# Transposed x by token tiles in DRAM and stored over six stages, attention tiles on the right side of SBUF, last stores on SyncE

## The chip, the cores and the metric

The kernel runs on one core of a Trainium2 chip. The metric is the device time of one execution in microseconds, the median over several executions. The timed number is about 1.8 us longer than the span of the same execution in its profile (for one execution of the changed kernel 1546.8 against 1545.1 us), so a span and a time are never compared with each other here.

## The reference

One transformer-like block on 2048 tokens of width 1024 in bf16: a layer norm, a segment-recurrent attention (32 heads of 128, segments of 32 tokens, 8 memory tokens carried from segment to segment), and an MLP-mixer branch, added to x. Cut to what matters here:

```python
def _A_ref(x, mem0, Wq, Wk, Wv, Wo, seg_len):      # x is the layer-normed input
    ...
    for s in range(n_seg):                         # 64 segments of 32 tokens
        h = concatenate([mem, xs], axis=1)         # 8 memory rows + 32 tokens
        q, k, v = h @ Wq, h @ Wk, h @ Wv           # 32 heads x 128
        p = softmax(mask(q k^T * scale))
        o = (p v) @ Wo
        mem = o[:, :M]
        outs.append(o[:, M:])
...
return x + _A_ref(xn, ...) + _B_ref(xn, w1, w2, w3, w4)
```

## The kernel before

The kernel has these stages, with their times in its trace: layer norm and the mixer branch (to about 545 us), the projection to V (545 to 771 us), attention in five groups of token blocks, (0), (1), (2), (3) and (4, 5), each over eight groups of heads (771 to about 1495 us), and the output projection with its closing checks. Four parts matter.

The V stage multiplies the transposed x, which lies in SBUF as `xT`, with eight slices of Wv. The results go through `Vs` buffers to DRAM on the SyncE queue. In the second of the eight steps the whole `xT` is also stored to DRAM, on the GpSimd queue, because its SBUF space is given up afterwards:

```python
vsp = vctx.enter_context(tc.tile_pool(name="vsp", bufs=3, side="right"))
...
for hg in range(8):
    ...                                            # loads of Wv, and of Wo for 1 <= hg < 5, on GpSimd
    for m4 in range(4):
        Vs = vsp.tile([P, 4, 512], BF16, tag="Vs")
        for j in range(4):
            ps = psum.tile([P, 512], F32, tag="mm", bufs=4)
            for k in range(KT):
                nc.tensor.matmul(ps[:], xT[:, m4 * 4 + j, k, :], wv[:, k, :], ...)      # L569
            if j % 2 == 0:
                nc.scalar.copy(Vs[:, j, :], ps[:])                                      # L571
            else:
                nc.vector.tensor_copy(Vs[:, j, :], ps[:])
        nc.sync.dma_start(V_d[...], Vs[:])
    if hg == 1:
        ...
        for n in range(NT):                        # 16 stores of 256 KB in a burst
            nc.gpsimd.dma_start(xT_d[:, :, n * P:(n + 1) * P], xT[:, n])                # L579
```

Attention reads the transposed x back, block by block of 384 tokens (the last block has 128), in 18 DMAs on GpSimd. `block_setup` for the next group is written in the third step of the group before, so almost a whole group ahead of its use:

```python
def block_setup(b):
    ...
    elif b == 5:
        nc.gpsimd.dma_start(hTb[:, :, 0:96], xT_d[:, :, a:a + 96])                      # L603
        nc.gpsimd.dma_start(hTb[:, :, 99:131], xT_d[:, :, a + 96:a + 128])              # L604
        nc.vector.tensor_copy(hTb[:, :, 96:99], MZ[:, :, 67:70])                        # L605
        nc.vector.tensor_copy(hTb[:, :, 131:132], MZ[:, :, 70:71])                      # L606
        ...
    else:
        for i in range(4):
            nc.gpsimd.dma_start(hTb[:, :, i, 0:96], xT_d[:, :, a + 96 * i:a + 96 * (i + 1)])   # L612
...
if hg == 2 and gi_ + 1 < len(groups):
    nextB = {b: block_setup(b) for b in groups[gi_ + 1]}
```

The two small copies at L605 and L606 put columns for the memory rows into the tile of block 5. They run on VectorE, which also does part of the softmax.

The weights of the next step of attention are loaded on SyncE, in two halves each, and SyncE also issues the transposes of the softmax weights P:

```python
for k0 in (0, 4):
    loads.append(lambda ...: nc.sync.dma_start(w[:, k0:k0 + 4, :], src[:, k0:k0 + 4, cs_]))    # L724
...
nc.sync.dma_start_transpose(PTr, Pn[:rows]...)                                          # L669
```

The results are stored on GpSimd, piece by piece, the last two pieces at the very end:

```python
nc.vector.tensor_tensor(ot[:], self.ps[:], self.Rt[:], op=ALU.add)                      # L703
nc.gpsimd.dma_start(out_v[:, self.gi, self.cc], ot[:])                                  # L704
```

Of the kernel before, what the change touches and what calls it, by code (L numbers as in the profile page):

```python
# [15 lines left out]
BF16 = mybir.dt.bfloat16  # L16
# [7 lines left out]
P = 128  # L24
S = 2048
D = 1024
KT = D // P
NT = S // P
# [49 lines left out]
def kernel(  # L78
# [16 lines left out]
    nc = tc.nc  # L95
    x_v = A_x[0].rearrange("(n p) d -> p n d", p=P)
    out_v = out[0].rearrange("(n p) d -> p n d", p=P)
# [12 lines left out]
    R1_v = R1_d.rearrange("(n p) d -> p n d", p=P)  # L110
    xn_d = tc.dram_tile([S, D], BF16, name="xn_scratch")
    xn_v = xn_d.rearrange("(n p) d -> p n d", p=P)
    xT_d = tc.dram_tile([P, KT, S], BF16, name="xT_scratch")
    V_d = tc.dram_tile([S, H * DH], BF16, name="V_scratch")
    Vr_d = tc.dram_tile([NQ + 1, H * DH], BF16, name="Vmem_scratch")

# [41 lines left out]
    def tiles_of(b):  # L158
        if b == 5:
            segs = (3, 1)  # L160
        else:
            segs = (3, 3, 3, 3)
        out_, c, t0 = [], 0, 4 * b
        for i, s in enumerate(segs):
            first = b == 0 and i == 0
            nm = s + (M - 1 if first else 0)
            msk = mask_first if first else (mask_reg if s == 3 else mask_last)
            r0 = 0 if first else 7 + 3 * (t0 + i)
            out_.append(dict(c0=c, ntok=s * SEG, nm=nm, T=s * SEG + nm, mask=msk, r0=r0, tok=i * 96, i=i, gi=t0 + i))
            c += s * SEG + nm  # L170
        return out_, c

    def fill(hTb, tl, x_of):

        for t in tl:
            a = t["tok"]
            end = a + t["ntok"]
            while a < end:
                j, o = divmod(a, P)
                w = min(P - o, end - a)  # L180
                d = t["c0"] + a - t["tok"]
                nc.vector.tensor_copy(hTb[:, :, d:d + w], x_of(j)[:, :, o:o + w])
                a += w
            d = t["c0"] + t["ntok"]
            nc.vector.tensor_copy(hTb[:, :, d:d + t["nm"]], MZ[:, :, t["r0"]:t["r0"] + t["nm"]])

    with tc.manual_schedule(engines={mybir.EngineType.PE, mybir.EngineType.SP, mybir.EngineType.Pool}), ExitStack() as actx:
        wpool = actx.enter_context(tc.tile_pool(name="aw", bufs=4, side="right"))

        def wtile():  # L190
            return wpool.tile([P, KT, 512], BF16, tag="w", name="wt")

        psum = actx.enter_context(tc.tile_pool(name="psum", bufs=4, space=PSUM))
        with ExitStack() as bctx:
# [13 lines left out]
            with ExitStack() as hctx:  # L208
# [161 lines left out]
                with ExitStack() as p2:  # L370
                    ring = p2.enter_context(tc.tile_pool(name="p2ring", bufs=4))
                    for n in range(NT):
                        x1 = ring.tile([P, D], F32, tag="x1")
                        st = ring.tile([P, 2, 6], F32, tag="st")
                        for ch in range(2):
                            ps = psum.tile([P, 512], F32, tag="mm", bufs=4)
                            for k in range(KT):
                                o = 2 + n * P + SH[k]
# [5 lines left out]
                        a = ring.tile([P, 1], F32, tag="a")  # L384
# [12 lines left out]
            with ExitStack() as p3:  # L397
# [97 lines left out]
                def load_wv():  # L495
                    hg = len(wvs)
                    if hg < 8:
                        wvs.append(wtile())
                        nc.gpsimd.dma_start(wvs[-1][:], Wv_v[:, :, hg * 512:(hg + 1) * 512])
# [10 lines left out]
                for tb in range(4):  # L510
# [12 lines left out]
                    if tb == 3:  # L523
# [4 lines left out]
                        xT = vph.tile([P, NT, KT, P], BF16)  # L528
                    for j in range(4):
                        n = tb * 4 + j  # L530
# [26 lines left out]
            for hg in range(8):  # L557
                cs_ = slice(hg * 512, (hg + 1) * 512)
                while len(wvs) < min(8, hg + 3):
                    load_wv()  # L560
                wv = wvs[hg]
                if 1 <= hg < 5:
                    nc.gpsimd.dma_start(wo_sb[:, (hg - 1) * 8:hg * 8, :], Wo_v[:, (hg - 1) * 8:hg * 8, :])
# [5 lines that stand above are left out]
                            nc.tensor.matmul(ps[:], xT[:, m4 * 4 + j, k, :], wv[:, k, :], start=(k == 0), stop=(k == KT - 1))  # L569
# [4 lines that stand above are left out]
                    nc.sync.dma_start(V_d[m4 * 512:(m4 + 1) * 512, cs_].rearrange("(j p) c -> p j c", p=P), Vs[:])  # L574
                if hg == 1:
                    for t in pns:
                        nc.gpsimd.memset(t[:], 0.0)
                    for n in range(NT):
                        nc.gpsimd.dma_start(xT_d[:, :, n * P:(n + 1) * P], xT[:, n])  # L579
                if hg == 6:  # L580
                    first_w = [wtile(), wtile()]
                    for w, src in zip(first_w, (Wq_v, Wk_v)):
                        nc.sync.dma_start(w[:], src[:, :, 0:512])
                if hg == 0:
                    tl, nb = tiles_of(0)
                    hTb0 = early.tile([P, KT, 408], BF16, tag="hTb")
                    fill(hTb0, tl, lambda j: xT[:, j])
# [3 lines left out]
        apsum = actx.enter_context(tc.tile_pool(name="apsum", bufs=2, space=PSUM))  # L591
        smp = actx.enter_context(tc.tile_pool(name="asm", bufs=2))
        iop = actx.enter_context(tc.tile_pool(name="aio", bufs=2))
        qkv = actx.enter_context(tc.tile_pool(name="aqkv", bufs=2))
        def block_setup(b):
            tl, nb = tiles_of(b)
            ntok = sum(t["ntok"] for t in tl)
            a = 384 * b
            if b == 0:
                hTb, rhs = hTb0, lambda k: hTb0[:, k, :nb]  # L600
            elif b == 5:
                hTb = early.tile([P, KT, 136], BF16, tag="hT5", bufs=1)
                nc.gpsimd.dma_start(hTb[:, :, 0:96], xT_d[:, :, a:a + 96])  # L603
                nc.gpsimd.dma_start(hTb[:, :, 99:131], xT_d[:, :, a + 96:a + 128])  # L604
                nc.vector.tensor_copy(hTb[:, :, 96:99], MZ[:, :, 67:70])  # L605
                nc.vector.tensor_copy(hTb[:, :, 131:132], MZ[:, :, 70:71])  # L606
                rhs = lambda k: hTb[:, k, :nb]
            else:
                hTb = early.tile([P, KT, 4, 104], BF16, tag="hTb")
                r0 = tl[0]["r0"]  # L610
                for i in range(4):
                    nc.gpsimd.dma_start(hTb[:, :, i, 0:96], xT_d[:, :, a + 96 * i:a + 96 * (i + 1)])  # L612
                nc.vector.tensor_copy(hTb[:, :, :, 96:99], MZ[:, :, r0:r0 + 12].rearrange("p k (t r) -> p k t r", t=4))
                rhs = lambda k: hTb[:, k, :, 0:99]
                for i, t in enumerate(tl):
                    t["c0"] = 104 * i
            return dict(b=b, tiles=tl, nb=nb, ntok=ntok, rhs=rhs, cols=nb if b in (0, 5) else 416)
# [67 lines left out]
        class Out:  # L685
            def __init__(self, oX, gi, gl, ch):
                self.oX, self.gi, self.gl, self.cc, self.ps = oX, gi, gl, slice(ch * 512, (ch + 1) * 512), None
                self.late = False

            def piece(self, hg):  # L690
                if self.ps is None:
                    self.ps = psum.tile([P, 512], F32, tag="mm", bufs=4, name="pso")
                if hg == (6 if self.late else 0):
                    self.Rt = iop.tile([P, 512], F32, tag="Rt")
                    nc.gpsimd.dma_start(self.Rt[:], R_v[:, self.gi, self.cc])
                for h in range(4 * hg, 4 * hg + 4):
                    nc.tensor.matmul(self.ps[:], self.oX[:, h, self.gl * P:(self.gl + 1) * P], wo_sb[:, h, self.cc], start=(h == 0), stop=(h == H - 1))  # L697
                if hg == 7:
                    ot = iop.tile([P, 512], BF16, tag="ot")
                    if DEBUG_A:  # L700
                        nc.vector.tensor_copy(ot[:], self.ps[:])
                    else:
                        nc.vector.tensor_tensor(ot[:], self.ps[:], self.Rt[:], op=ALU.add)  # L703
                    nc.gpsimd.dma_start(out_v[:, self.gi, self.cc], ot[:])  # L704

        smalls = []
        clock = [0.0]
# [21 lines left out]
        def tick(us, blocked=None):  # L729

            clock[0] += us
            turn[0] += 1
            if turn[0] % every == 0:
                load_some(1)
            done = set()
            for item in list(smalls):
                due, kind, fn = item
                if due <= clock[0] and kind != blocked and kind[0] not in done and not (kind[0] == "S" and flying[0] >= 5):
                    smalls.remove(item)
                    flying[0] += 1 if kind[0] == "S" else -1  # L740
                    done.add(kind[0])
                    clock[0] += fn()
# [57 lines left out]
        head, rest = outs[:4], outs[4:]  # L800
        for o in head:
            o.late = True
        for p in range(6):
            for o in head:
                o.piece(p)
                tick(0.86)
# [45 lines left out]
    with tc.If(cond > 0):  # L852
        with ExitStack() as fctx:
# [18 lines left out]
            with tc.For_i(0, NSEG, 1) as i:  # L872
# [57 lines left out]
                ot = fr.tile([L, D], BF16, tag="ot")  # L930
# [50 lines left out]
```

## Time and profile before

| | before |
|---|---|
| median of 3 runs at the time of the prediction | 1542.9 us (1540.59 to 1543.96) |
| TensorE busy | 1514.8 of 1545.1 us |
| sum of TensorE's gaps over 0.5 us | 16.0 us, in 12 gaps |
| largest of them | 3.37 us at 594 us, in the V stage |

The last two rows are worked out from the trace's list of weight loads: a gap is the time from the end of one weight load to the start of the next. The last matmul still runs for a part of it, so the idle time of TensorE is 0.1 to 0.4 us shorter: 3.08 us in the largest gap. The prediction's 16 us are the same sum. In the same way, all gaps named below without a profile line are gaps between weight loads.

In the profile's lines PE is TensorE at its matmuls, PEld TensorE loading weights, ACT ScalarE, DVE VectorE, POOL GpSimd, and SPq the DMA queue of SyncE. The page's head gives the span, and its first part the busy time, share of the span and number of instructions of each engine:

```profile
span 1545.1 us, 25390 instructions
PE 1514.8 (98%) x10308; PEld 839.7 (54%) x10382; DVE 523.8 (34%) x1092; ACT 513.9 (33%) x1218; POOL 192.5 (12%) x272
```

TensorE is the limit: only what takes gaps from it, or puts gaps into it, can move the time. The matmul count is 10308 although 10382 weights were loaded. Some matmul records are missing from this trace, so its PE sum is a little low and isn't compared with that of another trace.

The list of waits names the waiting engine and tile, then what released it, then total us, number, and the longest:

```profile
ACT Vs L571 <- DMA V_scratch<-Vs: 21.7, 3, 9.8
...
ACT QT L647 <- DMA V_scratch<-Vs: 4.9, 1, 4.9
...
PE ps L569 <- ACT Vs L571: 3.1, 1, 3.1
...
PE ps L639 <- DMA wt<-in_A_Wq_dram: 1.3, 2, 0.6
```

The first and third lines belong together. ACT couldn't evict a V result because a store from `Vs` to DRAM hadn't freed its buffer, and TensorE then waited for that eviction. The timeline of TensorE shows where (start, length, line, output and inputs, count, and in brackets the wait ahead), and the windows below it show each engine's busy time, then the granted clock (the share of full speed that TensorE was given), DMA share and GB/s. The four windows are two around this wait and two at 1215 to 1235 us:

```profile
584.70 9.44 PE L569 MATMUL ps<-wt,xT 128*128 128x512 bf16 x42
597.23 8.97 PE L569 MATMUL ps<-wt,xT 128*128 128x512 bf16 x32 [3.08 <-ACT Vs L571]
```

```profile
core 0: us, PE busy (x) PEld busy (x) DVE busy (x) ACT busy (x) POOL busy (x), PEclk, DMA share, GB/s
585.00:595.00 10.00, 9.09 (x42) 4.02 (x42) 1.38 (x2) 1.07 (x2) 0.00 (x0) 1.00 0.98 278
595.00:605.00 10.00, 7.72 (x28) 3.21 (x29) 1.98 (x3) 2.25 (x4) 0.00 (x0) 0.83 0.82 295
1215.00:1225.00 10.00, 10.00 (x82) 6.35 (x80) 3.09 (x7) 5.96 (x17) 6.36 (x8) 1.00 0.79 152
1225.00:1235.00 10.00, 10.00 (x77) 6.18 (x75) 6.82 (x17) 5.55 (x15) 0.00 (x0) 1.00 1.12 233
```

A clock of 0.83 over 10 us is 3.4 us at half clock; it follows the gap, and costs half of its length.

GpSimd's timeline shows the burst of stores that filled the DMA engines, and much later its loads of x for the last group:

```profile
553.22 5.26 POOL L579 DMA_DIRECT2D xT_scratch<-xT  x6
560.73 0.84 POOL L579 DMA_DIRECT2D xT_scratch<-xT  x1 [2.26 <-DMA wt<-in_A_Wv_dram]
568.61 0.84 POOL L579 DMA_DIRECT2D xT_scratch<-xT  x1 [7.04 <-DMA wo_sb<-in_A_Wo_dram]
569.89 3.46 POOL L579 DMA_DIRECT2D xT_scratch<-xT  x4 [0.43 <-issue]
...
1215.36 0.55 POOL L704 DMA_DIRECT2D out_dram<-ot  x1 [5.83 <-DVE ot L703]
1215.89 3.52 POOL L612 DMA_DIRECT2D hTb<-xT_scratch  x4
1219.41 0.88 POOL L603 DMA_DIRECT2D hTb<-xT_scratch  x1
1220.28 0.88 POOL L604 DMA_DIRECT2D hTb<-xT_scratch  x1
```

SyncE's timeline at that place has the second half of Wq, 1.8 us after the last of GpSimd's six loads was issued (1220.28 + 0.88 = 1221.16). This order was not noticed before the prediction:

```profile
1222.99 0.57 SPq L724 DMA_DIRECT2D wt<-in_A_Wq_dram  x1
```

At the end of the kernel, the lines of the output stores and of the closing drain (engine, operation, count, shortest/median/longest in ns, then first and last start):

```profile
L704 POOL DMA_DIRECT2D out_dram<-ot x32: 540/545/560, 901.1 to 1540.1; - x32
```

```profile
L976 POOLq DRAIN  x3: 46/98/3166, 1541.1 to 1544.9; - x3
```

GpSimd issues its last store at 1540.1 us and then drains for 3.17 us.

### The profile page before, as it was taken

How to read it: one execution, taken by the hardware profiler on the slowest of the kernel's cores; microseconds unless marked ns; L12 is line 12 of the kernel's file. 1: busy time of each engine (PE TensorE's matmuls, PEld its weight loads, DVE VectorE, ACT ScalarE, POOL GpSimd, SP SyncE). 2: the span in 40 equal slices, each digit the busy share in tenths (PEclk: the TensorE clock that was granted, in tenths of full speed). 3: DMA queues.
4: the chain of work that ended last, by engine and by line, in shares of the span. 5: the costliest groups of instructions: out<-in, count | busy, mean ns of one | idle time of the engine just before them, and what ended most of it. 6: DMA issues, size and time to landing. Idle time of an engine off the chain costs nothing. (4 is left out here: it accounts for less than half of the span.)

```text
span 1545.1 us, 25390 instructions
## 1 busy us (share of the span) xinstructions
PE 1514.8 (98%) x10308; PEld 839.7 (54%) x10382; DVE 523.8 (34%) x1092; ACT 513.9 (33%) x1218; POOL 192.5 (12%) x272
## 2 busy tenths in 40 slices
PE   7999999999999999999999999999999999999998
PEld 7844444444444444444456645654665566466654
DVE  8284010000200111111246624651663365235541
ACT  5533202103012011111156614651662366056620
POOL 5232020221211241010000011002000200100001
PEclk9999999999999999999999999999999999999999
DMA  7679543452353998542389947992997599458611
GB/s 251 182 213 311 205 148 125 143 184 83 130 164 87 215 275 273 173 124 83 123 231 252 235 129 179 246 237 73 239 239 175 129 249 227 111 130 198 136 45 50
DMA packets 288601, 270.39 MB, mean 175 GB/s; under 512 B 137459, under 2 KB 255368, under 8 KB 288480
## 3 DMA queue, kind: packets, MB, share of 16 engines
q1 hardware_dynamic: 265088, 185.53, 47.0%
q0 software_dynamic: 23392, 83.19, 16.8%
q8 instruction: 83, 1.36, 0.4%
q14 instruction: 38, 0.31, 0.1%
HBM read 190.73 MB, written 46.73 MB: 154 GB/s over the span
## 5 line engine op out<-in xcount | busy, mean ns | idle before, releaser
L639 PE MATMUL ps<-hTb,wt 128*128 128x396 bf16 (+2 forms) x3072 | 514.9, 314 | 1.3 <-DMA wt<-in_A_Wq_dram 1.3
L639 PEld LDWEIGHTS <-wt 128*128 128x128 bf16 x3072 | 264.5, 97 | 148.1 <-DMA wt<-in_A_Wq_dram 2.1
L569 PE MATMUL ps<-wt,xT 128*128 128x512 bf16 x1004 | 222.0, 381 | 4.1 <-ACT Vs L571 3.1
L697 PE MATMUL pso<-wo_sb,oX 128*128 128x512 bf16 x1000 | 223.2, 379 | 1.4 <-issue 0.2
L515 PE MATMUL ps<-xn3T,w_sb 128*128 128x512 bf16 x896 | 195.9, 379 | 1.1 <-ACT h3T L516 1.1
L540 PE MATMUL ps<-w_sb,h3T 128*128 128x512 bf16 x872 | 194.3, 379 | 1.2
L569 PEld LDWEIGHTS <-xT 128*128 128x128 bf16 x1024 | 100.6, 98 | 125.3 <-issue 5.6
L516 ACT ACTIVATE h3T<-ps 128x512 bf16<-128x512 f32 x112 | 66.5, 597 | 292.0 <-PE ps L515 289.0
L697 PEld LDWEIGHTS <-oX 128*128 128x128 bf16 x1024 | 98.9, 98 | 115.3
L645 ACT CAST KT<-ps 128x396 bf16<-128x396 f32 (+1 forms) x192 | 87.1, 456 | 189.6 <-PE ps L639 186.5
L515 PEld LDWEIGHTS <-w_sb 128*128 128x128 bf16 x896 | 86.8, 98 | 103.9 <-issue 1.3
L540 PEld LDWEIGHTS <-h3T 128*128 128x128 bf16 x896 | 86.8, 98 | 102.8
L660 DVE TENSOR_REDUCE sums<-sm 99x4 f32<-99x396 f32 (+1 forms) x176 | 97.6, 555 | 113.9 <-ACT sm L658 113.9
L647 ACT ACTIVATE QT<-ps 128x396 bf16<-128x396 f32 (+1 forms) x192 | 89.4, 469 | 108.0 <-PE ps L639 79.8
L656 DVE TENSOR_TENSOR sm<-psS,c_mask_reg_sb 99x396 f32<-99x396 f32 x160 | 91.4, 572 | 90.1 <-PE psS L654 89.9
L571 ACT CAST Vs<-ps 128x512 bf16<-128x512 f32 x64 | 37.2, 586 | 238.4 <-PE ps L569 152.6
L658 ACT ACTIVATE sm<-sm 99x396 f32<-99x396 f32 (+1 forms) x176 | 92.7, 527 | 65.9 <-DVE sm L656 64.7
L573 DVE CAST Vs<-ps 128x512 bf16<-128x512 f32 x64 | 44.2, 692 | 181.8 <-PE ps L569 156.8
L666 DVE TENSOR_TENSOR Pn<-sm,rs 99x396 bf16<-99x396 f32 (+1 forms) x176 | 99.0, 562 | 10.2 <-DMA PT<-Pn 4.0
L541 DVE TENSOR_TENSOR R<-ps,R 128x512 f32<-128x512 f32 x32 | 22.1, 692 | 231.4 <-PE ps L540 215.0
L704 POOL DMA_DIRECT2D out_dram<-ot x32 | 17.5, 546 | 575.8 <-DVE ot L703 569.9
L679 ACT CAST oX<-psO 128x384 bf16<-128x384 f32 x176 | 82.5, 469 | 16.8 <-PE psO L678 16.7
(116 smaller groups left out, 979.5 us busy)
## 6 DMA issues: line engine op xcount, KB each, us to landing
wt<-in_A_Wq_dram SPq DMA_DIRECT2D x78, 512.0 KB
wt<-in_A_Wk_dram SPq DMA_DIRECT2D x78, 512.0 KB
wt<-in_A_Wv_dram POOLq DMA_DIRECT2D x24, 1024.0 KB, 7.1
V_scratch<-Vs SPq DMA_DIRECT2D x32, 512.0 KB
V<-V_scratch SPq DMA_DIRECT2D x40, 384.0 KB
w_sb<-in_B_w_dram SPq DMA_DIRECT2D x9, 1024.0 KB
R_scratch<-x POOLq DMA_DIRECT2D x16, 512.0 KB, 4.4
R<-R_scratch SPq DMA_DIRECT2D x16, 512.0 KB
```

What stands on the lines that cost most here:

```text
L515: nc.tensor.matmul(ps[:].rearrange("p (n t) -> p n t", t=P), w3_sb[:, k, f * P:(f + 1) * P], xn3T[tb][:, :, k, :], start=(k == 0), stop=(k ...
L540: nc.tensor.matmul(ps[:], h3T[:, f, j * P:(j + 1) * P], w4_sb[:, f, ch * 512:(ch + 1) * 512], start=(f == 0), stop=(f == FT - 1))
L569: nc.tensor.matmul(ps[:], xT[:, m4 * 4 + j, k, :], wv[:, k, :], start=(k == 0), stop=(k == KT - 1))
L639: nc.tensor.matmul(ps[:, :nb] if B["b"] in (0, 5) else ps[:, :nb].rearrange("p (t c) -> p t c", t=4), w[:, k, hh * P:(hh + 1) * P], B["rhs ...
L645: nc.scalar.copy(o, i)
L647: nc.scalar.mul(o, i, scale)
L656: nc.vector.tensor_tensor(sm[:T, :, :T], S3, t["mask"][:].unsqueeze(1).to_broadcast((T, 4, T)), op=ALU.add)
L658: nc.scalar.activation(e[:T, :, :T], sm[:T, :, :T], ACTF.Exp, scale=LN2)
L660: nc.vector.tensor_reduce(ss, e[:T, :, :T], axis=AX.X, op=ALU.add)
L666: nc.vector.tensor_tensor(Pn[:T, :, :T], e[:T, :, :T], rs[:T, :].unsqueeze(2).to_broadcast((T, 4, T)), op=ALU.mult)
L679: nc.scalar.copy(oX[:, hs_, t["tok"]:t["tok"] + nt], O3[:, :, 0:nt])
L697: nc.tensor.matmul(self.ps[:], self.oX[:, h, self.gl * P:(self.gl + 1) * P], wo_sb[:, h, self.cc], start=(h == 0), stop=(h == H - 1))
```

## The change

It has four parts. (A) The DRAM copy of the transposed x is laid out by tiles of 128 tokens, so that a store writes runs of 2 KB and no longer of 256 B; a load must then be cut where it crosses a tile. (B) The stores are spread over six steps of the V stage, three each. (C) The attention tiles for V go to the right side of SBUF, meant to free attention's first V load from the V stage's buffers. (D) The last two output stores go to SyncE, meant to spare the end of the kernel GpSimd's drain. No arithmetic changes.

```diff
-    xT_d = tc.dram_tile([P, KT, S], BF16, name="xT_scratch")
+    xT_d = tc.dram_tile([NT, P, KT, P], BF16, name="xT_scratch")
@@ V stage
-                    for n in range(NT):
-                        nc.gpsimd.dma_start(xT_d[:, :, n * P:(n + 1) * P], xT[:, n])
+                if 1 <= hg < 7:
+                    for n in range(3 * hg - 3, min(NT, 3 * hg)):
+                        nc.gpsimd.dma_start(xT_d[n], xT[:, n])
@@ attention
-        qkv = actx.enter_context(tc.tile_pool(name="aqkv", bufs=2))
+        qkv = actx.enter_context(tc.tile_pool(name="aqkv", bufs=2, side="right"))
+        def load_tokens(dst, a, w):
+            while w:
+                n, o = divmod(a, P)
+                c = min(P - o, w)
+                nc.gpsimd.dma_start(dst[:, :, :c], xT_d[n, :, :, o:o + c])
+                dst, a, w = dst[:, :, c:], a + c, w - c
@@ block_setup
-                nc.gpsimd.dma_start(hTb[:, :, 0:96], xT_d[:, :, a:a + 96])
-                nc.gpsimd.dma_start(hTb[:, :, 99:131], xT_d[:, :, a + 96:a + 128])
+                load_tokens(hTb[:, :, 0:96], a, 96)
+                load_tokens(hTb[:, :, 99:131], a + 96, 32)
...
-                    nc.gpsimd.dma_start(hTb[:, :, i, 0:96], xT_d[:, :, a + 96 * i:a + 96 * (i + 1)])
+                    load_tokens(hTb[:, :, i, 0:96], a + 96 * i, 96)
@@ class Out  (self.last is False by default)
-                    nc.gpsimd.dma_start(out_v[:, self.gi, self.cc], ot[:])
+                    (nc.sync if self.last else nc.gpsimd).dma_start(out_v[:, self.gi, self.cc], ot[:])
@@ end of the kernel
+        for o in rest[-2:]:
+            o.last = True
```

A block of 384 tokens is loaded in four slices of 96, and two of these cross a tile border: six loads instead of four. Blocks 1 to 4 take 24 loads and block 5 two, 26 in all instead of 18.

More of the change, by code (lines that the diff above doesn't have):

```diff
@@ L687, in __init__ @@
                 self.oX, self.gi, self.gl, self.cc, self.ps = oX, gi, gl, slice(ch * 512, (ch + 1) * 512), None
-                self.late = False
+                self.late = self.last = False
             def piece(self, hg):
```

## The prediction

> **What bounds it now.** TensorE: the page's first part shows matmuls busy 1514.8 of 1545.1 us (98%). Its gaps over 0.5 us sum to 16 us: a change touching no matmul can win only microseconds.
>
> **Where the change meets a TensorE wait**
>
> 1. *V projection (545 to 771 us).* The list of waits: V matmuls waited 3.1 us for the ACT eviction of Vs, and ACT 9.8 us for a Vs store to free a buffer. Timeline: 594 to 597 us; then the granted clock is 0.5 for 3.4 us, another 1.7 us lost. The Trainium skill, "TensorE: Matmul & The Clock Gate", Part 1, describes this half clock after idleness; the trace agrees. Together 5 us.
> Cause: transposed x (16 x 256 KB, 256 B runs) is stored in one burst on the GpSimd queue from 553 us. That queue's 4096 B packets (190 to 300 ns) alternate with the Vs stores' 1024 B packets (50 to 60 ns), which leaves Vs about a fifth of the DMA time, some 60 GB/s, while V comes at 0.5 MB per 6.9 us (76 GB/s). "DMA: Bandwidth & Descriptors", Queues, rings and completion order, has engines take turns between queues by packet; the packet counts agree. The fourth Vs store took 17 us. The burst ran at 1 MB per 6.5 us, the weight loads of this queue at 3.2.
> The change stores three tiles (0.77 MB) in each of six stages, in 2 KB runs: an estimated 2.5 us of queue time a stage instead of over 20 at once. The queue should be idle from 567 to 573 us, the backlog drain, stall and half clock vanish: **-5 us**.
>
> 2. *Tail.* The last Vector add ends at 1539.84 us; GpSimd issues the last store, landed at 1542.5, but drains for 3.17 us, to 1544.3; the closing barrier ends at 1545.1. With the last two stores on SyncE, GpSimd drains earlier. SyncE then has the issue, its flag load and branch (2.07 us in this trace), beside the landing (2.0 us), 0.7 us of semaphores, 0.7 us of barrier: end near 1543.8, **-1.2 us**.
>
> 3. *V to attention (771 to 785 us).* Two TensorE waits for Wq (1.3 us): SyncE held the V load, and weights behind it, until the last Vs store landed at 775.5. The right side changes addresses, but by my sums of tile sizes the region still overlaps the Vs buffers by 3 KB, so I expect the wait to stay. Counted: **-0.3 us**.
>
> **What it adds.** Loads of transposed x go from 18 to 26 GpSimd issues of 0.88 us, some in 64 B runs, issued a block ahead on an engine 12% busy: 0. Waits for P transposes may shift by a microsecond.
>
> **Prediction: 1542.9 - 6.5 = 1536.4 us, range 1533.5 to 1540.5.** Faster by over 2% 0.01, within 2% 0.98, slower by over 2% 0.01.
>
> **What would show it.** 1: no TensorE wait for Vs near 590 us, clock 1.0 there; stores of x spread from 553 to about 720 us, landing in under 6 us. 2: no GpSimd issue after 1535 us, span end 4 us after the last Vector add. 3: first V load still released by the last Vs store.
>
> **What would make it wrong.** Weight and Wo loads (3 MB a stage) alone may starve the Vs stores; short-run loads may delay SyncE's loads in attention; the scheduler may reorder ACT and Vector; SyncE's branch may come later, losing the tail.

## The result, and the profile after

Each ratio below is the mean time of one kernel's runs over that of the other's runs of the same rounds, so it is not quite the ratio of the medians that stand beside it. Executions over 1.5% slower than the fastest of the same kernel are left out of the means. The brackets are the 95% interval.

| | before | after |
|---|---|---|
| median of 6 runs | 1542.38 us (1540.59 to 1544.17) | 1546.9 us (1545.2 to 1548.25) |
| ratio to before | | 1.0024 [1.001, 1.0038] |

The change made the kernel slightly slower, by 0.24%, inside the band of 2%. The predicted 1536.4 us and its whole range (up to 1540.5 us) were missed. The two profiles have the same span only because the profile of before caught one of its longer executions; a second profile of the same kernel has 1539.6 us. The second one is the yardstick in the table of stretches further down.

The head and first part of the page after:

```profile
span 1545.1 us, 25477 instructions
PE 1520.2 (98%) x10382; PEld 840.2 (54%) x10382; DVE 523.7 (34%) x1092; ACT 513.7 (33%) x1218; POOL 193.4 (13%) x278
```

Here all matmul records are present. The 5 us more of PE time are not more work: the weight loads, which are complete in both, took 839.7 and 840.2 us.

The waits that answer to those shown of before:

```profile
ACT QT L656 <- DMA V_scratch<-Vs: 4.9, 1, 4.9
...
PE ps L648 <- DMA wt<-in_A_Wq_dram: 3.3, 3, 1.9
...
PE psS L663 <- ACT KT L654: 2.4, 3, 1.9
```

The wait for `Vs` is gone. ACT's wait for the last `Vs` store is the same 4.9 us. New are 2.0 us more of waiting for Wq (3.3 us against 1.3), and waits for the eviction of K. The timeline and the windows show both places. TensorE now runs through the V stage at full clock, but stands idle at 1225 us. A half clock follows, 6.8 us of it in this profile:

```profile
584.73 21.53 PE L569 MATMUL ps<-wt,xT 128*128 128x512 bf16 x99
```

```profile
585.00:595.00 10.00, 10.00 (x48) 4.55 (x47) 2.07 (x3) 1.75 (x3) 0.00 (x0) 1.00 0.60 226
595.00:605.00 10.00, 10.00 (x48) 4.50 (x46) 1.97 (x3) 1.75 (x3) 3.43 (x5) 1.00 0.40 119
1215.00:1225.00 10.00, 10.00 (x75) 6.08 (x73) 2.46 (x5) 3.25 (x8) 4.28 (x6) 1.00 0.82 181
1225.00:1235.00 10.00, 5.72 (x25) 2.96 (x25) 6.29 (x16) 4.56 (x12) 0.00 (x0) 0.73 0.76 186
```

```profile
1224.32 0.84 PE L648 MATMUL ps<-hTb,wt 128*128 128x396 bf16 x4
1227.07 0.85 PE L648 MATMUL ps<-hTb,wt 128*128 128x396 bf16 x4 [1.92 <-DMA wt<-in_A_Wq_dram]
...
1230.74 0.24 PE L663 MATMUL psS<-KT,QT 128*99 128x99 bf16 x1 [1.93 <-ACT KT L654]
```

The first group of four matmuls uses the first half of Wq. The second half isn't there, and TensorE waits 1.92 us for it. The 1.93 us for ACT come by a second way, over VectorE. Here is the copy of L605, first before, then after (where it is L614):

```profile
1225.69 0.19 DVE L605 COPY hTb<-MZ 128x24 bf16<-128x24 bf16 x1 [1.72 <-DMA hTb<-xT_scratch]
```

```profile
1225.74 0.18 DVE L614 COPY hTb<-MZ 128x24 bf16<-128x24 bf16 x1 [6.81 <-DMA hTb<-xT_scratch]
```

The copy waits for block 5's loads of x to land. VectorE does nothing else meanwhile, so the softmax behind the copy is late. On ScalarE an exp of that softmax stands in front of the eviction of K for which TensorE waits until 1230.74 us:

```profile
1229.78 0.54 ACT L667 ACTIVATE sm<-sm 99x396 f32<-99x396 f32 x1 [1.22 <-DVE sm L665]
1230.22 0.47 ACT L654 CAST KT<-ps 128x396 bf16<-128x396 f32 x1
```

GpSimd and SyncE at this place:

```profile
1211.17 0.55 POOL L713 DMA_DIRECT2D out_dram<-ot  x1 [6.69 <-issue]
1211.71 7.01 POOL L601 DMA_DIRECT2D hTb<-xT_scratch  x8
```

```profile
1217.95 0.58 SPq L733 DMA_DIRECT2D wt<-in_A_Wq_dram  x1
```

The eight loads were issued from 1211.71 to 1218.72 us, and the half of Wq at 1217.95 us: 0.77 us before the end of these issues, where before it came 1.8 us after. The stores and loads of x, with the issue costs (shortest/median/longest in ns) and first and last start; then the output stores and the closing drain, in the same columns:

```profile
L601 POOL DMA_DIRECT2D hTb<-xT_scratch x26: 880/883/904, 660.1 to 1217.8; - x26
L580 POOL DMA_DIRECT2D xT_scratch<-xT x16: 540/556/572, 553.0 to 659.5; - x16
```

```profile
L713 POOL DMA_DIRECT2D out_dram<-ot x30: 540/545/567, 896.2 to 1526.8; - x30
L713 SPq DMA_DIRECT2D out_dram<-ot x2: 356/367/378, 1533.8 to 1540.7; - x2
```

```profile
L987 POOLq DRAIN  x3: 51/98/3688, 1528.9 to 1544.8; - x3
```

GpSimd's long drain now starts at 1528.9 us, 12 us earlier, and is over before the last two stores.

### Where the time went

The 10,382 weight loads have the same order in all traces, so each trace can be laid beside another, load by load, and the difference in elapsed time be read for each stretch. The table gives it in microseconds against the second profile of before (column 2 is the V stage around the burst, columns 3 and 4 lie in attention and after it). The last column is a length of its own: from the end of the last Vector add to the end of the span. From 610 to 770 us every trace agrees within 0.1 us, and from 770 to 1215 us they differ by -0.7 to +3.2 us without a pattern. Single executions of any kernel differ by up to 4 us in the column "1245 to end", mostly in waits for transposes of P.

| profile of | 545 to 610 | 1215 to 1245 | 1245 to end | end |
|---|---|---|---|---|
| before (first) | +0.6 | +0.3 | +3.4 | 5.29 |
| before_again (yardstick) | 0 | 0 | 0 | 5.30 |
| after | -4.4 | +7.6 | +1.9 | 4.38 |
| after_again | -4.4 | +6.8 | +3.5 | 3.99 |

So the V stage gave nearly what was predicted, and the end of the kernel 0.9 to 1.3 us. Both were paid for by a stall at 1225 us. Laid load by load beside the kernel before, its 7.6 us are 4.9 us of waiting (the two gaps of 2.32 and 2.01 us with two short waits for K between them) and 2.7 us at half clock. The half clock lasts 6.8 us but costs less than half of that, since 1.2 us of it lie in the second gap.

The record keeps a second profile of each of four kernels: before_again, dram_layout_and_spread, right_side_only and last_stores_on_sync_only. It was not used for the table. Where it says something else than the first, this is said below.

### The profile page after: what moved, and what is told of

The parts are those of the page before. It is cut to its first block, busy times and chain, and to the rows that moved or that the text cites. A ratio compares the mean times of both kernels' runs of the same rounds, so it can differ in the third digit from the quotient of the medians.

```text
span 1545.1 us, 25477 instructions
## 1 busy us (share of the span) xinstructions
PE 1520.2 (98%) x10382; PEld 840.2 (54%) x10382; DVE 523.7 (34%) x1092; ACT 513.7 (33%) x1218; POOL 193.4 (13%) x278
## 4 chain that ended last, share of the span: by engine, by line
PE 93%; DMA 3%; DVE 1%; ACT 1%; POOL 1%; issue 0%; SPq 0%; ACTq 0%; DVEq 0%; POOLq 0%
PE ps L648 27%; PE pso L706 14%; PE ps L569 14%; PE ps L540 13%; PE ps L515 12%; PE ps L379 4%; PE ps L300 3%; PE psS L663 2%; PE psO L687 2%; DMA PT<-Pn 1%; DMA xn2T<-xn 1%; PE ps L832 1%; PE gps L446 1%; PE ps L466 1%; PE ps L432 1%; DMA hTb<-xT_scratch 1%
```

## The experiments

The theory after the first look: the eight cut loads take GpSimd longer to issue and put more into the DMA engines just when SyncE asks for the second half of Wq, and that half is late. Three rivals could be held against it: it is the place or form of the new DRAM copy (part A) that slows the transfers, not their number; it is the right side of SBUF (part C) that moves waits; or it is one execution's accident. All kernels here gave correct results. The 16 runs went to the chip in four calls of four; the runs of a call share the runs of the kernel before, whose median is given for each call.

### First call: the parts alone (before: 1544.91 us)

**before_again** is the kernel before, unchanged, to see what the comparison makes of no change.

```diff
(no edit)
```

> The kernel before, unchanged, to see what varies between its executions. Its first profile had a 5 us event in the V projection (3.1 us stall near 594 us plus 3.4 us of half clock), yet its profiled execution was of 1545.1 us, about 4.5 us longer than its timed runs suggest. Theory 1: the event is in most executions, so this profile shows it again (gap over 2.5 us between 585 and 600 us) and the ratio is 1.000. Rival: the event belongs to that one execution; this profile has no such gap and a span near 1541 us, which would explain why my predicted 5 us were not there to win.

Measured: ratio 0.9997 [0.9981, 1.0014], 1543.14 us, span 1539.6 us. The V stage's gap is 2.81 us with 3.4 us at half clock again, so this stall is no accident of the first profile. The kernel's second profile has a gap of 2.83 us but no half clock.

**dram_layout_and_spread** has A and B alone.

```diff
+ xT_d by tiles, load_tokens, stores over six steps (as in the change)
- side="right";  - last two stores on SyncE
```

> Only the DRAM part: transposed x by token tiles, stored over six stages, 26 loads. Theory 1 (the loads in attention, in short runs and in eight pieces before the last group, delay SyncE's weights near 1225 us by about 4 us plus 3.4 us of half clock): ratio 1.002 to 1.005, the gap near 1225 us present. Rival (the right side or the SyncE stores cost it): ratio 0.997 to 1.001.

Measured: ratio 1.001 [0.9995, 1.0025], 1546.47 us. V stage -4.4 us, 1215 to 1245 us +7.1 us. Both the gain and the loss are in A and B. This rules out part C and part D as the source of the stall.

**right_side_only** has C alone.

```diff
-        qkv = actx.enter_context(tc.tile_pool(name="aqkv", bufs=2))
+        qkv = actx.enter_context(tc.tile_pool(name="aqkv", bufs=2, side="right"))
```

> Only the attention tiles on the right side: same sizes, addresses moved by 2272 bytes. Theory 1: 1.000 within 0.001, the first V load still waits for the last Vs store. Rival (addresses matter): 1.002 to 1.004.

Measured: ratio 1.0022 [1.0005, 1.0039], 1547.4 us, with executions from 1542.46 to 1551.61 us; span 1540.7 us. The interval excludes 1, yet the profile shows no stretch in which it loses: 1215 to 1245 us is 0, and ACT's wait for the last `Vs` store is there as before. The V stage has its gap of 2.93 us, but this time without the half clock, as two lines for the window from 595 to 605 us show, first of before_again, then of this kernel:

```profile
595.00:605.00 10.00, 9.21 (x35) 3.87 (x36) 2.45 (x4) 2.25 (x4) 0.21 (x1) 0.83 0.73 266
```

```profile
595.00:605.00 10.00, 9.95 (x46) 4.53 (x47) 2.02 (x4) 2.06 (x4) 1.76 (x2) 1.00 0.78 272
```

So a gap of 2.8 to 2.9 us is followed by the half clock in one execution and not in another, and 1.7 us of the stall's price come and go. (The second profile has a gap of 3.08 us, again without it.)

**last_stores_on_sync_only** has D alone.

```diff
-                    nc.gpsimd.dma_start(out_v[:, self.gi, self.cc], ot[:])
+                    (nc.sync if self.last else nc.gpsimd).dma_start(out_v[:, self.gi, self.cc], ot[:])
+        for o in rest[-2:]:
+            o.last = True
```

> Only the last two stores on the SyncE queue. Theory 1: ratio 0.9994 (about -0.9 us; from the last matmul to the end 5.6 us instead of 6.5 us). Rival (SyncE's branch comes late): 1.000 to 1.001.

Measured: ratio 1.0003 [0.9988, 1.0018], 1544.67 us. The end of the kernel after the last Vector add is 4.73 us instead of 5.30. That is 0.6 us, which the timed runs don't resolve. The second profile has 4.13 us, a gain of 1.2 us.

### Second call: what in A and B does what (before: 1543.77 us)

**spread_only** has B alone: the old layout with its runs of 256 B and its uncut loads, but three stores a step.

```diff
-                    for n in range(NT):
-                        nc.gpsimd.dma_start(xT_d[:, :, n * P:(n + 1) * P], xT[:, n])
+                if 1 <= hg < 7:
+                    for n in range(3 * hg - 3, min(NT, 3 * hg)):
+                        nc.gpsimd.dma_start(xT_d[:, :, n * P:(n + 1) * P], xT[:, n])
```

> Old DRAM layout and old 18 loads; only the stores of transposed x spread over six stages. Theory 1 (the V stall comes from the burst; the gap near 1225 us comes from the eight loads before the last group reaching past the issue of the second half of Wq): no gap over 1 us near 594 us, none near 1225 us, ratio 0.9965 to 0.9985. Rival (spreading itself, or the DRAM tiles, disturbs the attention stage): the gap near 1225 us is there.

Measured: ratio 0.9966 [0.9934, 0.9998], 1538.88 us. V stage -4.4 us, and 0 at 1215 to 1245 us. The predicted gain in the V stage is real, and it shows in the time when nothing is lost elsewhere.

**tiles_only** has A alone: the new layout and cut loads, but all 16 stores in the second step.

```diff
-                        nc.gpsimd.dma_start(xT_d[:, :, n * P:(n + 1) * P], xT[:, n])
+                        nc.gpsimd.dma_start(xT_d[n], xT[:, n])
+ load_tokens (as in the change)
```

> New layout and 26 loads, but all 16 stores in one burst as before, now in 2 KB runs. Theory 1: gap of 4 to 5 us plus half clock near 1225 us present; near 594 us the stall is smaller or gone because the burst takes about 13 us instead of 26 us; ratio 1.001 to 1.004. Rival (spreading is what hurts): no gap near 1225 us.

Measured: ratio 1.0003 [0.9961, 1.0044], 1543.05 us. V stage -4.4 us as well: runs of 2 KB take the stall away without any spreading, so A and B each suffice and don't add up. At 1215 to 1245 us it loses 1.8 us. The stall is there but milder than in the full change, without a half clock.

**old_layout_split_loads** is the kernel before with only its loads cut, from the old layout, at the same tokens.

```diff
+                nc.gpsimd.dma_start(dst[:, :, :c], xT_d[:, :, a:a + c])    # in load_tokens, old xT_d
-                    nc.gpsimd.dma_start(hTb[:, :, i, 0:96], xT_d[:, :, a + 96 * i:a + 96 * (i + 1)])
+                    load_tokens(hTb[:, :, i, 0:96], a + 96 * i, 96)
```

> The kernel before with its old layout and burst, but its 18 loads cut into 26 at the same 128 token borders. Theory 1 (number and shape of the loads): gap near 1225 us appears, 4 to 5 us with half clock, V stall stays, ratio 1.003 to 1.006. Rival (the place in DRAM, 192 B runs read 256 B apart instead of 4 KB apart): no gap near 1225 us, ratio 1.000 within 0.0015.

Measured: ratio 1.0035 [0.9993, 1.0077], 1548.26 us. V stage 0, and +4.1 us at 1215 to 1245 us, with gaps of 0.61 and 2.02 us and 3.4 us at half clock. The two waits in its trace:

```profile
1228.47 0.85 PE L647 MATMUL ps<-hTb,wt 128*128 128x396 bf16 x4 [0.21 <-DMA wt<-in_A_Wq_dram]
...
1231.45 0.24 PE L662 MATMUL psS<-KT,QT 128*99 128x99 bf16 x1 [1.93 <-ACT KT L653]
```

The half of Wq is hardly late here, yet TensorE waits as long for K as in the changed kernel: VectorE's copy waited 4.41 us for the loads of block 5. The new layout isn't needed for the stall: cutting the loads at the same tokens is enough, and the place in DRAM is not the cause. A cut makes more loads and shorter runs at once, though, and this run doesn't part the two.

**after_loads_two_stages_later** is the changed kernel with the loads written two steps later, to pull them away from the half of Wq.

```diff
-                if hg == 2 and gi_ + 1 < len(groups):
+                if hg == 4 and gi_ + 1 < len(groups):
```

> The whole change, but the loads of transposed x are issued at the fifth head group of a block instead of the third, away from the Wq half that is issued late. Theory 1 (collision in time): gap near 1225 us gone, V stall gone, ratio 0.9965 to 0.9985 to before, about 7 us below the changed kernel. Rival (the loads cost the same wherever they stand): a gap of 4 us elsewhere, ratio 1.001 to 1.003.

Measured: ratio 1.0018 [0.9987, 1.0049], 1547.19 us, +6.2 us at 1215 to 1245 us. The experiment missed its aim. In its trace the loads run at 1212.94 us, again right behind the last output store (1212.40 us). GpSimd gets to them when that store is done, wherever between two stores they are written. So it says nothing on what other timing would do. It does show that "issued a block ahead" in the program is not a time on the chip.

### Third call: take the two extra loads away from that place (before: 1544.01 us)

**after_block5_loaded_early** is the changed kernel with block 5 set up in the first group, so that six loads and not eight come before the last group. The loads stay cut and the layout stays new.

```diff
-                    nextB = {b: block_setup(b) for b in groups[gi_ + 1]}
+                    nextB = {b: B5 if b == 5 else block_setup(b) for b in groups[gi_ + 1]}
+                    if gi_ == 0:
+                        B5 = block_setup(5)
```

> The whole change, but the two loads of block 5 are issued with those of block 1, near 660 us, so that six loads instead of eight stand before the last group. (In the last batch, writing the loads two stages later in the program did not move them in time: GpSimd reached them right behind the last output store, at 1212.9 us, and the event stayed.) Theory 1 (eight loads at 0.88 us each reach past the issue of the Wq half): GpSimd's last load issue ends 1 us or more before the Wq half is issued, no TensorE gap over 1 us between 1215 and 1245 us, ratio 0.996 to 0.998 to before. Rival (the short 64 B runs slow the Wq half whatever their time): a gap of 1 to 2.5 us stays, ratio 0.999 to 1.002.

Measured: ratio 0.9989 [0.9969, 1.0008], 1542.2 us, span 1536.7 us. V stage -4.4 us, 1215 to 1245 us 0. The loads and the half of Wq in its trace, and the only wait for Wq left, which is the one at 777 us:

```profile
1208.00 0.55 POOL L713 DMA_DIRECT2D out_dram<-ot  x1 [4.97 <-DVE ot L712]
1208.54 5.28 POOL L601 DMA_DIRECT2D hTb<-xT_scratch  x6
```

```profile
1215.63 0.58 SPq L733 DMA_DIRECT2D wt<-in_A_Wq_dram  x1
```

```profile
PE ps L648 <- DMA wt<-in_A_Wq_dram: 0.6, 1, 0.6
```

The issues end at 1213.82 us, 1.8 us before the half of Wq is asked for, as in the kernel before, and TensorE doesn't wait. VectorE's two copies have also left this place, together with the loads of block 5. The six executions fall into two groups, though, of 1538.46 to 1540.43 and 1543.97 to 1545.89 us. The profile is of one of the faster group, so what the slower ones lose isn't seen.

**after_without_right_side** and **after_again** are a direct pair for part C: the changed kernel without and with it.

```diff
-        qkv = actx.enter_context(tc.tile_pool(name="aqkv", bufs=2, side="right"))
+        qkv = actx.enter_context(tc.tile_pool(name="aqkv", bufs=2))
```

> The whole change without the move to the right side. Theory 1 (the move does nothing): equal to the whole change in this call within 0.001; event near 1225 us present. Rival (the move itself costs 0.002, as its lone run read): 0.002 below the whole change.

> The whole change once more, on the chip of this call, as the partner of the two runs above. Both theories: gap of 2 us twice near 1225 us with half clock, none near 594 us, ratio 1.001 to 1.004.

Measured: without, 1.0007 [0.9991, 1.0023], 1545.17 us; with, 1.0012 [0.9996, 1.0028], 1546.43 us. At 1215 to 1245 us they lose 6.1 and 6.8 us. The pair shows no effect of the right side, and the 1.0022 of the lone run found no support; as no stretch of its profile explains it, it is held for scatter, but that is not proved. The changed kernel is again no faster than before, so its result wasn't an accident.

**spread_sync_block5_early** leaves the old layout and the uncut loads, and takes B, D and the early block 5.

```diff
+ stores over six steps, old xT_d (as in spread_only)
+ last two stores on SyncE (as in the change)
+ B5 = block_setup(5) in the first group (as in after_block5_loaded_early)
```

> A candidate to beat both: old DRAM layout and uncut loads, stores of transposed x spread over six stages, last two stores on SyncE, block 5 loaded early so that four loads stand before the last group. Theory 1: no gap near 594 us and none over 1 us near 1225 us, from the last matmul to the end 5.6 us; ratio 0.9955 to 0.998. Rival (256 B runs spread over the stage cost elsewhere): 0.999 or more.

Measured: ratio 0.9963 [0.9948, 0.9978], 1538.88 us, span 1536.2 us. It beats the kernel before and the changed one of the same call. V stage -4.4 us, 0 at 1215 to 1245 us, end 4.73 us. With four loads ahead of the last group GpSimd issues them in 3.53 us.

### Fourth call: is the cut harmless where there is room (before: 1543.27 us)

**block5_early_again** and **block5_early_third_look** repeat after_block5_loaded_early; the third look is one profile and one time.

```diff
(as after_block5_loaded_early)
```

> The whole change with block 5 loaded early, once more. In the last call half of its executions took 1538.5 to 1540.4 us and half 1544 to 1546 us at a lower clock. Theory 1 (six cut loads end only 1.8 us before the Wq half is issued, so the event near 1225 us comes in some executions): two groups of times again; a profile at 1544 us or more shows a gap near 1225 us, one at 1540 us or less shows none. Rival (the slow executions have another cause): a slow profile without a gap near 1225 us.

> The same kernel, one more look for its profile. Same expectation as the run before it.

Measured: ratio 0.9978 [0.9956, 1.0001], 1541.65 us, spans 1538.8 and 1536.0 us, one time of 1537.72 us. At 1215 to 1245 us +0.7 and 0. In three profiles of three the event is gone or nearly so. No profile fell into the slower group of executions, so that question stays open.

**old_layout_spread_sync_b5_cut_loads** is spread_sync_block5_early with cut loads from the old layout: 26 loads, but six ahead of the last group.

```diff
 (spread_sync_block5_early)
+ load_tokens with the old xT_d (as in old_layout_split_loads)
```

> The best candidate (old layout, spread, SyncE, block 5 early), with its loads cut at the 128 token borders. Theory 1 (cutting makes the loads long, whatever the layout): some executions slow again, ratio 0.998 to 1.000, like the whole change with block 5 early. Rival (the new layout is what costs there): as fast as the uncut one, 0.9955 to 0.9975.

Measured: ratio 0.9953 [0.9931, 0.9975], 1538.47 us, 0 at 1215 to 1245 us. It is as fast as the uncut one. Block 4 is still cut here into the same six pieces as in the change, four of them short, so neither the cut nor the short runs cost anything by themselves. It costs where eight loads instead of six stand in front of the half of Wq.

**before_block5_early** is the control: the kernel before with only the early block 5.

```diff
 (before)
+ B5 = block_setup(5) in the first group (as in after_block5_loaded_early)
```

> The kernel before with only block 5 loaded early: four loads instead of six before the last group, the V stall stays. Theory 1 (six uncut loads leave the Wq half just enough time in nearly all executions): no gain, 0.9985 to 1.0005. Rival (before, too, has the event near 1225 us in many executions): 0.996 to 0.998.

Measured: ratio 1.0004 [0.9972, 1.0036], 1544.02 us, V stage -1.8 us (the gap of 2.72 us without a half clock), 0 at 1215 to 1245 us. Loading block 5 early is no gain of its own. It only removes a stall that the kernel before doesn't have.

### What the runs say together

The stretches of all kernels, in microseconds as in the table above; "loads" is the number of loads of x ahead of the last group, and an end left blank was not measured in this way:

| profile of | loads | 545 to 610 | 1215 to 1245 | half clock near 1235 | end |
|---|---|---|---|---|---|
| before_again | 6 | 0 | 0 | none | 5.30 |
| spread_only | 6 | -4.4 | 0 | none | 5.32 |
| last_stores_on_sync_only | 6 | -0.1 | 0 | none | 4.73 |
| tiles_only | 8 | -4.4 | +1.8 | none | |
| old_layout_split_loads | 8 | 0 | +4.1 | 3.4 | |
| after_without_right_side | 8 | -4.4 | +6.1 | 3.4 | 4.17 |
| after_again | 8 | -4.4 | +6.8 | 6.8 | 3.99 |
| dram_layout_and_spread | 8 | -4.4 | +7.1 | 6.8 | |
| after | 8 | -4.4 | +7.6 | 6.8 | 4.38 |
| after_block5_loaded_early | 6 | -4.4 | 0 | none | 4.36 |
| old_layout_spread_sync_b5_cut_loads | 6 | -4.4 | 0 | none | |
| spread_sync_block5_early | 4 | -4.4 | 0 | none | 4.73 |

All seven profiles with eight loads have the stall (the seventh, of after_loads_two_stages_later, lost 6.2 us), and none of the eleven with six or four lost more than 0.7 us there. The second profiles agree: 7.4 us with eight loads, and nothing in the three with six.

The traces show two ways from the loads to TensorE. In the table the landing is read from the half of Wq's own semaphore. The data are what the packets of GpSimd's DMA queue still had to move when the half was issued; with eight loads they include a load of 0.26 MB for the output sum (`Rt`), which GpSimd issues right behind the loads of x. For the four kernels named above the second profile was used:

| kernels | half of Wq, issue to landing | GpSimd's data after that issue | VectorE's copy waited |
|---|---|---|---|
| four loads | 3.7 and 3.9 us | none | no copy here |
| six loads, block 5 early | 4.3 us (old layout), 5.8, 6.3 and 7.0 us (new layout) | 0.19 to 0.22 MB | no copy here |
| six loads, as in before | 4.8 to 5.4 us | 0.22 to 0.23 MB | 1.1 to 1.7 us |
| tiles_only, old_layout_split_loads | 7.6 and 7.4 us | 0.52 MB | 3.7 and 4.4 us |
| eight loads, spread stores (five) | 8.7 to 9.6 us | 0.66 to 0.68 MB | 6.3 to 7.4 us |

Where the half is in time, TensorE starts on it 6.9 us after its issue. So it is late in the last two rows alone, and in block5_early_again, whose 7.0 us are the longest of the new layout, it comes at the last moment.

Why the stall is milder in the first two of the eight-load kernels is seen in part. In tiles_only GpSimd has a small unexplained pause of 0.76 us ahead of its load of `Rt` at 1197.14 us, two output stores earlier than in the changed kernel. The wait for the Vector add ahead of the next store absorbs it, the following store is on time (1209.65 us), and the eight loads run from 1210.19 to 1217.20 us. In the changed kernel the output store starts at 1211.17 us after "issue", with no wait that the profile shows, 0.76 to 0.86 us later against TensorE's progress, and pushes the eight loads closer to the half of Wq. What makes this pause fall there isn't shown by any run.

## Why the prediction was wrong

**V stage, predicted -5 us: right.** It was -4.4 us in all twelve profiles whose stores are spread or tiled, against a profile of before with gap and half clock (2.81 us + half of 3.4 us = 4.5 us). Against the second profile of before_again, which has no half clock, it is -2.7 us. The cause was right too, as spread_only and tiles_only show: the Trainium skill, "DMA: Bandwidth & Descriptors", Queues, rings and completion order, has the DMA engines take turns between queues by packet, and taking the burst away, or making it shorter, lets the `Vs` stores through. That turn-taking was not tested by itself. Three details were off. The stores were all issued by 659.5 us and not by about 720, since GpSimd ran ahead of TensorE. They took 8.5 to 16.6 us to land and not under 6. And a good third of the price, the clock, comes and goes. The Trainium skill, "TensorE: Matmul & The Clock Gate", Part 1, has a free-running window of about 3.4 us decide this, and the runs agree as far as they go: here the half clock lasted 3.4 us or twice that, and the length of the gap alone doesn't decide. Gaps of 2.81 and 2.75 us were followed by it, gaps of 2.93 and 2.72 us weren't. The page asks for at least one idle window of that length, though, and all these gaps are shorter.

**Tail, predicted -1.2 us: right.** It was 5.3 us from the last Vector add to the end, and is 4.0 to 4.4 us in the changed kernel, a gain of 0.9 to 1.3 us; with D alone it is 0.6 us in one profile and 1.2 us in another.

**V to attention, predicted -0.3 us with the wait left as it is: right about the wait.** The first V load is still released by the last `Vs` store and ACT still waits 4.9 us, which fits the overlap of about 3 KB that the prediction worked out; no trace shows addresses. No gain was found.

**"What it adds. Loads of transposed x go from 18 to 26 GpSimd issues of 0.88 us, some in 64 B runs, issued a block ahead on an engine 12% busy: 0." This step failed.** The number of loads and the 0.88 us were right; the 0 was wrong. It measured +7.6 and +6.8 us in the two profiles of the changed kernel, at 1215 to 1245 us. Two thoughts in it were mistaken.

- *"A block ahead"* was true of when TensorE needs the data, and beside the point. What counts is what the loads stand beside when they are issued, and who waits for them first. GpSimd reaches all of them at once, right behind the last output store. SyncE then asks for the second half of Wq, which TensorE needs about 7 us later (issued at 1217.95, waited for from 1225.16 us). And VectorE's copies into block 5's tile wait until block 5's loads have landed, 6.81 us in the changed kernel against 1.72 before, with the softmax behind them. So for VectorE the loads were late.
- *"12% busy"* is a mean over 1545 us. In these 7 us GpSimd is busy without a break. A load takes 0.88 us to issue whether it brings 96 tokens or 32, so eight take 7.0 us and six 5.3 us. The Trainium skill, "Perfetto Trace Analysis", DMA Instruction — SWDGE (GPSIMD), says that such a bar ends when the descriptors are made and not when the data have landed; so a load that was just issued can still be moving its data when the bar ends. The trace agrees: in the changed kernel the last of the eight loads landed 7.9 us after its issue began. The half of Wq, asked for 0.77 us before the last of the eight issues ended, was late, and asked for 1.8 us after the last of six it wasn't.

The prediction named a related risk, "short-run loads may delay SyncE's loads in attention". The delay came, and on the half of Wq, but it is only one of the two ways, and short runs alone aren't enough for it: with block 5 loaded early, the same short pieces of block 4 stand at the same place and the half is in time. The number of issues fits all 18 profiles. It is not fully parted from its companions. An early block 5 takes two issues away from this place, but also 0.26 MB and VectorE's two copies. No run had short runs and all the bytes with six issues, and none moved the copies alone. So how much of the stall goes over Wq and how much over VectorE is read from the traces and not tested.

**The size of the stall** in the changed kernel is 2.2 us over Wq, 2.7 us over K, and 2.7 us at half clock, which turns 4.9 us of waiting into 7.6 us.

**The sum.** For after_again the three terms are -4.4 + 6.8 - 1.3 = +1.1 us, and its ratio of 1.0012 is +1.9 us; for the first runs of after they are -4.4 + 7.6 - 0.9 = +2.3 us, and the ratio of 1.0024 is +3.7 us. The rest of about 1 us has the right size for the half clock in the V stage of before, which only some of its executions have (1.7 us each), but it is well within the scatter and is not attributed.

**What stays open:** why GpSimd's pause of 0.8 us falls before the last output store in some kernels and earlier in others; the slower group of executions of after_block5_loaded_early; and whether the new layout with an early block 5 (0.9989, 0.9978) is truly slower than the old layout with it (0.9963, 0.9953). They stood side by side in two calls, each time about 0.25% apart with overlapping intervals. The half of Wq points the same way: with the same six pieces of x in front of it, it took 5.8 to 7.0 us to land in the three profiles of the new layout and 4.3 us in that of the old. With TensorE needing it at 6.9 us, the new layout has little room; whether this makes the slower executions isn't shown.

## What to carry to other kernels

Cost an added DMA issue where it will run, not by its engine's mean load: find in the trace the instruction it will stand behind, and what other queue asks for data in the microseconds after it. Ask also which small instruction waits for the loaded data first, and what stands behind it on its engine: here two copies on VectorE held up the softmax. Where each piece of a split DMA costs the same to issue, as here, splitting lengthens the burst by that cost for each piece, even when the bytes stay the same. The clock that follows can add half as much again to the waits. When a gain is confirmed in its own stretch but the total doesn't move, align the two traces on an unchanged sequence of instructions and look for the stretch that gave it back.

## What the Trainium skill lacked or had wrong

- "DMA: Bandwidth & Descriptors", Anatomy of one DMA — SWDGE (gpsimd) path, calls descriptor generation "small, variable" and says that many descriptors can be emitted before the cost shows. Here it mattered: 0.88 us of GpSimd's time for each load of x, the same for 96 and for 32 tokens, and 7.0 us for eight in a row. A store of 256 KB took 0.56 us in runs of 2 KB and 0.84 us or more (0.90 us in the median) in runs of 256 B. The number of runs fits these figures and the bytes don't: the loads and the store in 256 B runs have 128 x 8 runs each, the store in 2 KB runs has 128.
- The same page, Issuing engines are not separate DMA queues, says that the sequencer time to initiate a DMA is usually small relative to the DMA itself. Here 1.7 us more of such time (seven against 5.3 us) before one load on another engine was worth up to 7.6 us. A word on the order of issue between engines is lacking.
- "TensorE: Matmul & The Clock Gate", Why this matters for your kernels, advises against idle gaps of over about 3 us. Here two gaps between weight loads of 1.9 to 2.8 us, less than 2.1 us apart, brought 3.4 or 6.8 us at half clock in five profiles of kernels with eight loads, gaps of 0.61 and 2.02 us brought 3.4 us in a sixth, and single gaps of 2.75 and 2.81 us brought 3.4 us, while one of 2.93 us brought none. Shorter gaps count as well, above all when two come close together.
- No page that was read here has the closing drain of GpSimd: 3.17 us after its last DMA issue in the kernel before, 3.69 us in the changed one, where it is hidden because it starts 12 us earlier.
- No page explains GpSimd's pause of 0.76 to 0.86 us without any visible wait, which decided in part how large the stall was.
